# Scores of the first 22 chunks as spread tiles with a second mix, loads of the first batch in halves, and a shorter first AV and F1 part

## The chip, the cores and the metric

The kernel runs on one core of a Trainium2 chip. The metric is the device time of one execution, in microseconds (us). The core's engines run their own instruction lists side by side and wait for each other by semaphores: TensorE (PE, with its weight loads PEld), VectorE (DVE), ScalarE (ACT), GpSimd (POOL) and SyncE (SP). Most loads are issued by POOL, the moves between on-chip tiles by SP.

## The reference

Talking-heads attention over 8 batches of 12 heads, 448 positions and 64 dimensions, and then a feed-forward network with a squared ReLU (d_model 768, d_ff 2048). The two small 12x12 matrices mix the heads before and after the softmax.

```python
scores = scale * np.matmul(q, k.transpose(0, 1, 3, 2))
scores = np.einsum('bhij,hg->bgij', scores, w_pre)
scores = scores - np.max(scores, axis=-1, keepdims=True)
attn = np.exp(scores)
attn = attn / (np.sum(attn, axis=-1, keepdims=True) + 1e-09)
attn = np.einsum('bhij,hg->bgij', attn, w_post)
out = np.matmul(attn, v)
x = out.transpose(0, 2, 1, 3).reshape(B * S, H * D)
h = np.maximum(x @ w_in, 0.0)
return h * h @ w_out
```

## The kernel before

Each batch's 448 query positions are cut into 45 chunks of 10 (CH; ND = 22 and NCH = 45 count chunks). A chunk's 10 positions times 12 heads make 120 rows of a tile, so one matmul with a block matrix of w_pre mixes the heads of a chunk.

The work of PE is made of units, and the units form ten streams, by the digits of the string ORDER: 0 transposes of q and k (T), 1 scores q k^T (QK), 2 the mix with w_pre (pre), 3 the mix with w_post together with a transposition (post), 4 attention times v (AV), 5 direct scores of the first chunks (dir), 6 and 7 the first feed-forward product (F1), 8 and 9 the second (F2). ORDER gives the order of PE's units by hand; within a stream they run in the order in which the program makes them. A planner in the program (`_Plan`, costs written beside each task) takes PE's order as given, places the work of the other engines around it, gives evictions marked FLEX to DVE or ACT, whichever is done first, and puts warm-up matmuls (L649) into early gaps of PE. PE's order is fixed in the program that results: a unit that waits holds back those behind it.

The usual way of a chunk is long: QK (L974, or L986 in 64x64 tiles) writes scores into PSUM, DVE or ACT copies them to `stage` (L526, L527), SP moves each chunk's rows by DMA into `dring` (L1029), pre (L1052) mixes them, ACT takes exp with its row sums (L1070) into `pring`, DVE inverts the sums (L1094), POOL (DVE for the first chunks) folds them into the w_post block (L1101), post (L1133) writes the mixed attention, and DVE or ACT copies it to `a2t`. Then AV (L1211), F1 (L1257, later L1278 and L1292), relu and square, and F2 (L1413, L1427).

The first batch does its first 22 chunks on another way, without `stage` and `dring`: `emit_scale` (L900, on DVE) multiplies q by w_pre for every output head and writes the scaled q into the still unused `w_out_sb` (16 chunks) and `h2t` (6 chunks); `emit_direct` (L922) then needs six full 128x128 matmuls of 448 columns per chunk, one for each pair of heads, and exp reads their sum from PSUM. `wq` (L613), made from `wall`, holds the scaled w_pre, and `init9` (L882, ACT) clears the rows of padding. The w_out loads (`emit_load_w(1, ...)`) wait until the 16 chunks have left `w_out_sb`.

The loads of the first batch: the first q comes by SP as float32 into `xt` and is cast (`first_q`), the other q and the three k by POOL with a cast on the way; then w_in's first quarter, v, q and k of batch 1, and the rest of w_in. `emit_T` transposes q or k of four heads by 28 small transposes (L821) and evicts them by two copies of 128x448 into `qkt`.

AV of the first batch has two parts, chunks 0 to 21 and 22 to 44 (PARTS0), and F1 one group for each.

Of the kernel before, what the change touches and what calls it, by code (L numbers as in the profile page):

```python
# [8 lines left out]
DT = mybir.dt  # L9
# [16 lines left out]
EVENTS = {"tr": 0.12, "qk": 0.72, "di": 0.2, "po": 0.61, "pr": 1.1, "av": 0.43, "o0": 0.43}  # L26
# [5 lines left out]
    "0001501510105151555555555555555551335510015555555553335510021551355553255310055511255321"  # L32
    "5551233232444133433367232276761132761316772121776333626422444333277721166331766111672227"
    "6633672033720921193932194002442002831831181218214338313812182128216661333662227776332276"
    "7633377412144331411762216776200227677333772338311821802083320026662422441761181118333831"
    "3831921292193342219321922393292194114442336316316136202072372273763336217227163360071002"
    "7183138112823811933292292191183328212833181424433434224441326213636131637112727200726162"
    "1727317200736336302091911291129128238331833182911292219233914244332422831831833284241244"
    "1236331617333701206362172373272373263001620062161271171291329223933913813382128121842144"
    "4338332842244421861162383163361173372721772007272172623636330064144422820081118139138139"  # L40
    "3319329229219223933811938318132842444132621621721726236316316337337272272761762821383388"
    "33832184244439382829229639363637672722767673386376474448767667677676767968989989889899"
# [329 lines left out]
def bass_talking_heads_attention__then__ffn_squared_relu_kernel(  # L372
# [19 lines left out]
    NDW = 16  # L392
    DH = 4
    NE = 6
    NQ0 = 2
    QT0 = tuple((CH * (ND + x * (NCH - ND) // NQ0),
# [13 lines left out]
    PARTS0 = ((0, HC[0]), (HC[0], NCH))  # L410
# [6 lines left out]
    with ExitStack() as es:  # L417
# [43 lines left out]
        wq = early_bf[:, 512:512 + NP * NR // 2].rearrange("p (n h a) -> p n h a", n=NP, h=H)  # L461
        wall = early[:, 512:512 + NP * 2 * H].rearrange("p (n x h) -> p n x h", n=NP, x=2)
# [21 lines left out]
        sem_hq = Sm("dhq")  # L484
# [3 lines left out]
        sem_wq = Sm("dwq")  # L488
# [34 lines left out]

        def copy(eng, en, o, i_):
            if en == ACT:
                return eng.activation(o, i_, AF.Copy)  # L526
            return eng.tensor_copy(o, i_)  # L527

        streams = [[] for _ in range(10)]
        plan.streams = streams  # L530
        s_T, s_QK, s_pre, s_post, s_AV, s_dir = streams[:6]
        s_F1, s_F2 = streams[6:8], streams[8:]
# [3 lines left out]
        def fn_init(eng, en):  # L536
            eng.memset(mask[:, :, :], 1.0)
            eng.memset(wk1[:, :], 0.0)
            eng.memset(wrep[:, :], 0.0)
            eng.memset(wk2b[:, :, :], 0.0)  # L540
            return eng.memset(ident[:, :], 0.0)
# [43 lines left out]
        t_zrow = add("zrow", DVE, lambda eng, en: eng.memset(zrow[0:R0, :], 0.0), [],  # L585
# [14 lines left out]
        def fn_wall(eng, en):  # L600
            src = bass.AP(w_pre.tensor, 0, [[0, 128], [1, H * H]])
            eng.dma_start(wall[:, :, :, :].rearrange("p a b c -> p (a b c)"), src).then_inc(
                sem_wq.handle, 16)
            return None

        t_wall = plan.add("wall", SP, fn_wall, [], {SP: (400.0, 5300.0)}, -1e6 - 1, sem_wq, 16)
        wq_of = []
        for kk in range(2):
            def fn_wq(eng, en, r0=kk * 64, kk=kk):
                r_ = None  # L610
                for u in range(2):
                    i_ = wall[r0:r0 + 64, kk:NP:2, u, :].unsqueeze(3).to_broadcast([64, 3, H, H5])
                    r_ = eng.tensor_scalar(wq[r0:r0 + 64, 3 * u:3 * u + 3, :, :], i_,  # L613
                                           scale, None, op0=ALU.mult)
                return r_

            wq_of.append(add("wq%d" % kk, DVE, fn_wq, [t_wall], {DVE: (560.0, 640.0)}, -2e6))
# [57 lines left out]
        def load_qk(b, a, x, u, deps, after, prio):  # L675
            raw, src = ((qraw, q), (kraw, k))[x]

            def fn(eng, en):
                h = b * H + 4 * a
                if b == 0:  # L680
                    i_ = bass.AP(src.tensor, h * S * D, [[2 * NT * D, 128], [1, 2 * NT * D]])
                    o = raw[:, 2 * a:2 * a + 2, :, :].rearrange("p c t d -> p (c t d)")
                else:
# [3 lines left out]
                eng.dma_start(o, i_).then_inc(sem_qk[a][x].handle, 16)  # L687

            return plan.add("ldqk%d_%d_%d_%d" % (b, a, x, u), POOL, fn, deps,
                            {POOL: (600.0, 0.0)}, prio, sem_qk[a][x], 16, after=after,  # L690
                            dma=("load", 700.0, 88.0) if b else ("load", 1100.0 if a else 2590.0, 165.0))

        def first_q():
            part = xt.bitcast(DT.float32)[:, 0:4, :].rearrange("p a s -> p (a s)")

            def fn(eng, en):
                i_ = bass.AP(q.tensor, 0, [[2 * NT * D, 128], [1, 2 * NT * D]])
                eng.dma_start(part, i_).then_inc(sem_hq.handle, 16)
                return None

            t = plan.add("hq", SP, fn, [], {SP: (400.0, 3400.0)}, -1e6 - 2, sem_hq, 16)
# [99 lines left out]
        def emit_T(b):  # L801
            pb = b % 2
            for a in range(3):
                g = _Group(2)
                trs = []
                for i, src in enumerate((qraw, kraw)):
# [30 lines left out]
                    if b:  # L837
                        continue
# [852 lines left out]
```

## Time and profile before

| | |
|---|---|
| median of 3 runs | 519.81 us (518.43 to 520.98) |
| span of the profiled execution | 520.6 us |
| granted TensorE clock, mean | 0.999 |
| PE busy | 505.5 us, 97% |
| ACT busy | 425.6 us, 82% |
| DVE busy | 398.7 us, 77% |
| HBM read, written | 45.70 MB, 11.01 MB |

The span runs from the first to the last instruction of the profiled execution. Matmuls are pipelined, so the duration of one (a mean of 354 ns for L922) is longer than its pitch from start to start; costs on PE have to be taken from start times. Busy time of an engine in a stretch counts overlapping instructions once. The chain of waits follows the work that ended last back to the start, and says for each piece what released it.

### The profile page before, as it was taken

The page shows a single profiled execution, that of the slowest core. Times are in us where ns is not written, and L with a number is a line of the kernel's source. Part 1 is how long each engine was busy: PE and PEld are TensorE (multiplying, and loading weights), DVE is VectorE, ACT ScalarE, POOL GpSimd, SP SyncE. Part 2 cuts the span into 40 slices and gives each one's busy share as a digit, 9 for nine tenths or more (in the row PEclk, how much of TensorE's full clock was granted, in tenths as well). Part 3 has the DMA queues.
Part 4 walks back from the last instruction along what each step waited for, and adds up shares of the span by engine and source line. Part 5 has one row for each costly group of instructions (what it writes and reads, how often), then busy time and mean ns, then how long its engine had stood idle before and what let it go on. Part 6 is the DMA issues. An engine that isn't in the chain of part 4 may idle for free.

```text
span 520.6 us, 25670 instructions
## 1 busy us (share of the span) xinstructions
PE 505.5 (97%) x10859; PEld 340.1 (65%) x10859; DVE 398.7 (77%) x1004; ACT 425.6 (82%) x1206; POOL 203.4 (39%) x404
## 2 busy tenths in 40 slices
PE   8999999899999999999999999999999999999996
PEld 4555777668766665667657665667666666678963
DVE  6967988789987869967997779976887669757430
ACT  4799999879998898989887999988788879878311
POOL 9914364325632384134622464225440333123010
PEclk9999999999999999999999999999999999999999
DMA  8999999646893699347974689457972568432013
GB/s 160 208 218 184 197 194 184 156 107 144 167 180 86 136 177 197 92 112 166 178 156 90 153 175 179 98 111 170 167 151 59 125 140 148 91 81 69 4 39 90
DMA packets 82724, 72.12 MB, mean 139 GB/s; under 512 B 13578, under 2 KB 80090, under 8 KB 82602
## 3 DMA queue, kind: packets, MB, share of 16 engines
q0 software_dynamic: 36944, 32.81, 38.5%
q1 hardware_dynamic: 45370, 37.38, 29.7%
q8 instruction: 89, 1.46, 1.1%
q14 instruction: 33, 0.27, 0.1%
q10 hardware_dynamic: 288, 0.20, 0.1%
HBM read 45.70 MB, written 11.01 MB: 109 GB/s over the span
## 4 chain that ended last, share of the span: by engine, by line
PE 92%; DMA 3%; DVE 2%; issue 2%; ACT 1%; POOL 0%; DVEq 0%
PE ps L1413 17%; PE ps L1278 12%; PE ps L1427 9%; PE ps L1292 9%; PE ps L1133 8%; PE ps L1052 8%; PE ps L1257 6%; PE ps L1211 6%; PE ps L922 5%; PE ps L974 4%; DMA dring<-stage 3%; PE ps L825 2%; PE ps L1362 2%; PE ps L986 2%; PE ps L649 1%
## 5 line engine op out<-in xcount | busy, mean ns | idle before, releaser
L1070 ACT ACTIVATE pring<-ps 128x448 bf16<-128x448 f32 x360 | 192.0, 550 | 12.6 <-PE ps L1052 7.3
L1101 POOL TENSOR_TENSOR wk2s<-wk2b,rinv 128x120 bf16<-128x120 bf16 (+1 forms) x179 | 69.0, 389 | 223.5 <-DVE rinv L1094 222.8
L527 DVE CAST a2t<-ps 128x480 bf16<-128x480 f32 (+1 forms) x201 | 122.1, 640 | 18.4 <-PE ps L1133 16.9
L527 DVE CAST stage<-ps 128x448 bf16<-128x448 f32 (+1 forms) x189 | 112.8, 618 | 19.0 <-PE ps L986 8.7
L526 ACT ACTIVATE stage<-ps 128x448 bf16<-128x448 f32 (+1 forms) x171 | 87.9, 549 | 18.2 <-PE ps L986 10.6
L526 ACT ACTIVATE a2t<-ps 128x480 bf16<-128x480 f32 x167 | 88.2, 570 | 15.5 <-PE ps L1133 15.0
L1413 PE MATMUL ps<-w_out_sb,h2t 64*128 64x384 bf16 x1056 | 95.9, 322 | 0.0
L1070 ACT ACTIVATION_READ_ACCUMULATOR pring<-ps 128x1 f32 x360 | 76.9, 214 | 0.0
L1133 PEld LDWEIGHTS ps<-wk2s,pring 60*128 60x128 bf16 x2880 | 54.9, 93 | 24.7 <-issue 5.8
L1278 PE MATMUL ps<-xt,w_in_sb 64*128 64x448 bf16 (+2 forms) x840 | 70.6, 309 | 0.0
L1413 PEld LDWEIGHTS ps<-w_out_sb,h2t 64*128 64x128 bf16 x1056 | 48.4, 94 | 31.1 <-PE ps L1052 0.7
L1459 POOL DMA_DIRECT2D out_dram<-osb x59 | 36.9, 632 | 75.9 <-DVE osb L527 25.8
L1133 PE MATMUL ps<-wk2s,pring 60*128 60x60 bf16 x2880 | 62.3, 187 | 1.9 <-issue 1.4
L1052 PE MATMUL ps<-dring,wk 64*64 64x448 bf16 (+1 forms) x676 | 61.5, 359 | 2.4 <-issue 1.2
L1427 PE MATMUL ps<-w_out_sb,h2t 64*64 64x384 bf16 x1216 | 57.4, 323 | 0.9 <-issue 0.8
L1323 DVE TENSOR_SCALAR h1t<-ps 128x448 bf16<-128x448 f32 (+2 forms) x96 | 46.2, 488 | 12.6 <-PE ps L1278 9.1
L1292 PE MATMUL ps<-xt,w_in_sb 64*64 64x448 bf16 (+1 forms) x1008 | 54.5, 345 | 0.8 <-issue 0.6
L1332 DVE TENSOR_TENSOR h2t<-h1t 128x448 bf16<-128x448 bf16 (+2 forms) x176 | 52.0, 331 | 1.4 <-ACT h1t L1322 0.9
L1322 ACT ACTIVATE h1t<-ps 128x448 bf16<-128x448 f32 (+2 forms) x80 | 35.4, 448 | 19.7 <-PE ps L1278 13.9
L1094 DVE RECIPROCAL rinv<-rowsum 128x2 f32<-128x2 f32 (+1 forms) x184 | 29.3, 160 | 28.2 <-ACT pring L1070 27.1
L1278 PEld LDWEIGHTS ps<-xt,w_in_sb 64*128 64x128 bf16 x840 | 38.3, 94 | 18.1 <-DVE rinv L1094 0.5
L1427 PEld LDWEIGHTS ps<-w_out_sb,h2t 64*64 64x64 bf16 x1216 | 38.2, 107 | 13.8 <-issue 2.0
(70 smaller groups left out, 595.0 us busy)
## 6 DMA issues: line engine op xcount, KB each, us to landing
dring<-stage SPq DMA_DIRECT2D x309, 105.0 KB
out_dram<-osb POOLq DMA_DIRECT2D x45, 192.0 KB, 3.7
qraw<-in_q_dram POOLq DMA_DIRECT2D x42, 112.0 KB, 5.3
kraw<-in_k_dram POOLq DMA_DIRECT2D x42, 112.0 KB, 6.2
w_in_sb<-in_moe_w_in_dram POOLq DMA_DIRECT2D x8, 384.0 KB, 16.3
w_out_sb<-in_moe_w_out_dram POOLq DMA_DIRECT2D x8, 384.0 KB, 11.9
vraw<-in_v_dram POOLq DMA_DIRECT2D x21, 128.0 KB, 4.8
vraw<-in_v_dram POOLq DMA_DIRECT2D x21, 96.0 KB, 5.0
```

The costliest lines, as they stand in the source:

```text
L526: return eng.activation(o, i_, AF.Copy)
L527: return eng.tensor_copy(o, i_)
L1052: r_ = eng.matmul(ps[64 * y:64 * y + 64, gr.banks[x], 0:S], wk1[64 * x:64 * x + 64 - R0 * x, :], dring[64 * x:64 * x + 64 - R0 * x, (g0 + ...
L1070: return eng.activation(pring[:, pr, 0:S], ps[:, gr.banks[x], 0:S], AF.Exp, accum_out=rowsum[:, rs, :])
L1101: return eng.tensor_tensor(wk2s[:, p0:p0 + n, :], i0.to_broadcast([128, n, PR]), rinv[:, p0:p0 + n, :].to_broadcast([128, n, PR]), ALU.mult)
L1133: r_ = eng.matmul(ps[:, gr.banks[x], o0:o0 + PR], pring[64 * x:64 * x + PR, pr + y, j0:j0 + 2 * PJ], wk2s[64 * x:64 * x + PR, pr + y, :], ...
L1278: r_ = eng.matmul(ps[:, g.banks[x], 0:n], w_in_sb[64 * y:64 * y + 64, ft, t * 128:(t + 1) * 128], xt[64 * y:64 * y + 64, ft, c0:c1], start ...
L1292: r_ = eng.matmul(ps[64 * z:64 * z + 64, g.banks[x], 0:n], w_in_sb[64 * y:64 * y + 64, ft, t:t + 64], xt[64 * y:64 * y + 64, ft, c0:c1], s ...
L1323: return eng.tensor_scalar(h1t[:, box[0], 0:n], ps[:, g.banks[x], 0:n], 0.0, None, op0=ALU.max)
L1332: return eng.tensor_tensor(h2t[:, t16, o0:o0 + n], h1t[:, box[0], 0:n], h1t[:, box[0], 0:n], ALU.mult)
L1413: r_ = eng.matmul(ps[:, g.banks[hh], 0:FH], h2t[64 * y:64 * y + 64, t16, col:col + 128], w_out_sb[64 * y:64 * y + 64, t16, hh * FH:(hh + 1 ...
L1427: r_ = eng.matmul(ps[64 * z:64 * z + 64, g.banks[hh], 0:FH], h2t[64 * y:64 * y + 64, t16, col + 64 * z:col + 64 * z + 64], w_out_sb[64 * y ...
```

## The change

Spread scores. `emit_scale`, `emit_direct`, `wq` and `wall` go. The transposed q of the first 22 chunks is evicted straight into `qs`, in `w_out_sb`, where each chunk has four column strips of 32: ten columns for each of three heads, with zeros at the places that don't belong to a strip's head. `emit_spread` makes per chunk eight matmuls of 128 rows and 32 columns (sx, stream 5), which leave the scores of the twelve heads in four strips of one PSUM bank, one eviction `sv` of 128x448 on DVE or ACT into `sring` (8 slots), and one full matmul with `wks`, a block matrix of w_pre (mx, a new stream a). exp reads mx's result.

Loads. q of the first batch comes in halves, the first ones (the first seven of the fourteen positions that a partition holds, which become the first 224 columns) among the k, the second ones after all k; the first half q and the first k come by SP as float32 and are cast; eight small DMAs (`wreps`) replace `wall`. Then `EARLY`: w_in's first quarter, v, q and k of batch 1, the rest of w_in. w_out's loads wait for the mx of all 22 chunks. The output rows of the first batch are permuted to suit.

Parts. AV of the first batch has three parts, chunks 0 to 13, 14 to 21 and 22 to 44, and F1 two groups, the first of 14 chunks (140 columns), the second of the rest (308 columns).

ORDER is another one, of 967 units for 966; some costs of the planner are changed.

```diff
+TL = 4
+EARLY = ("w0", "v", "qk0", "qk1", "qk2", "w1", "w2", "w3")
-PARTS0 = ((0, HC[0]), (HC[0], NCH))
+PARTS0 = ((0, 14), (14, HC[0]), (HC[0], NCH))
+GROUPS0 = (PARTS0[:1], PARTS0[1:])
...
 ORDER = (
-    "0001501510105151555555555555555551335510015555555553335510021551355553255310055511255321"
-    "5551233232444133433367232276761132761316772121776333626422444333277721166331766111672227"
...
+    "00000000115015111155555aaa15aaa555a15533aa5a55353aaa30aaa5533553444111aaa50240aaa7630713"
+    "2336661202047241134162217632427332337263327331637241144411162276773337226671316226613173"
...
+        def fn_wreps(eng, en):
+            for j in range(TL):
+                for c, n, h in ((0, 2, head(j, 0)), (2, 1, head(TL + j // 2, j % 2))):
+                    src = bass.AP(w_pre.tensor, h * H, [[2 * H, n], [0, CH], [1, H]])
+                    r0 = 32 * j + c * CH
+                    eng.dma_start(wreps[r0:r0 + n * CH, :], src).then_inc(sem_ws.handle, 16)
...
+        def fn_wks(eng, en):
+            r_ = None
+            for x in range(2):
+                o = wks[:, 64 * x:64 * x + PR].rearrange("p (b a) -> p b a", a=H5)
+                i0 = wreps[:, :].unsqueeze(2).to_broadcast([128, H, H5])
+                i1 = masks[:, x * H5:(x + 1) * H5].unsqueeze(1).to_broadcast([128, H, H5])
+                r_ = eng.scalar_tensor_tensor(o, i0, scale, i1, op0=ALU.mult, op1=ALU.mult)
+            return r_
...
+        def emit_load_qk(b, heads=range(3)):
+            n = 0
+            if b == 0:
+                for a, x, u in ((0, 0, 0), (0, 1, 0), (1, 0, 0), (1, 1, 0), (2, 0, 0), (2, 1, 0),
+                                (0, 0, 1), (1, 0, 1), (2, 0, 1)):
+                    if a == 0 and u == 0:
+                        t = first(x)
+                    else:
+                        t = load_qk(b, a, x, u, [], [chain["t"]], -1e7 + 2 * a + u)
+                        chain["t"] = t
+                    qk_tasks[(a, x, u)] = t
+                return
...
+        flat = w_out_sb[:, :, :].rearrange("p a b -> p (a b)")
+        nqs = ND * TL * 2 * 32
+        qs = flat[:, 0:nqs].rearrange("p (c j x k) -> p c j x k", j=TL, x=2, k=32)
+        sring = flat[:, nqs:nqs + NSR * S].rearrange("p (n s) -> p n s", n=NSR)
+        def fn_init9(eng, en):
+            z = zrow[:, 0:2].bitcast(DT.float32)
+            return eng.activation(flat[:, 0:nqs].bitcast(DT.float32),
+                                  z.to_broadcast([128, nqs // 2]), AF.Copy)
...
+                    def fn_ev(eng, en, u=u, p=p):
+                        r_ = None
+                        if ND * CH < w:
+                            r_ = copy(eng, en, qkt[:, 0, p, 0, ND * CH:w],
+                                      ps_bf[:, g.banks[0], u * w + ND * CH:(u + 1) * w])
+                        for x in range(2):
+                            rows = slice(64 * x, 64 * x + 64)
+                            j, part, o0 = (p, 0, x * CH) if p < TL else (
+                                2 * (p - TL) + x, 1, 2 * CH)
+                            r_ = copy(eng, en, qs[rows, :, j, part, o0:o0 + CH],
+                                      ps_bf[rows, g.banks[0], u * w:u * w + ND * CH].rearrange(
+                                          "p (c a) -> p c a", a=CH))
+                        return r_
...
+        def emit_spread(c):
+            g = _Group(1)
+            slot = c % NSR
+            def fn_sx(eng, en):
+                r_ = None
+                for part in range(2):
+                    for j in range(TL):
+                        p = TL + j // 2 if part else j
+                        r_ = eng.matmul(ps[32 * j:32 * j + 32, g.banks[0], 0:S],
+                                        qs[:, c, j, part, :], qkt[:, 0, p, 1, :],
+                                        start=(part == 0), stop=(part == 1))
+                return r_
+            t = unit(s_spr, "sx%d" % c, fn_sx,
+                     [trev[(0, p, 0)] for p in range(NP)] + [trev[(0, p)] for p in range(NP)],
+                     395.0, "c32", g, 2 * TL)
+            def fn_sv(eng, en):
+                return copy(eng, en, sring[:, slot, :], ps[:, g.banks[0], 0:S])
+            t_sv = add("sv%d" % c, FLEX, fn_sv, [t, dir_done.get(c - NSR)], c_ev(S), -500.0 + c)
+            g.readers[0].append(t_sv)
+            g2 = _Group(1)
+            def fn_mx(eng, en):
+                return eng.matmul(ps[:, g2.banks[0], 0:S], wks[:, :], sring[:, slot, :],
+                                  start=True, stop=True)
+            t_mx = unit(s_mix, "mx%d" % c, fn_mx, [t_sv, t_wks], 190.0, "full", g2, 1)
...
-                emit_load_w(1, [dir_done[c] for c in range(NDW)])
-                emit_load_v(b)
+                emit_load_w(1, [dir_done[c] for c in range(ND)])
...
-            groups = [(p,) for p in parts_of(b)] if b in split else [parts_of(b)]
+            groups = GROUPS0 if b == 0 else [(p,) for p in parts_of(b)] if b in split else [parts_of(b)]
```

More of the change, by code (lines that the diff above doesn't have):

```diff
@@ L539, in fn_init @@
             eng.memset(wrep[:, :], 0.0)
+            eng.memset(wreps[:, :], 0.0)
+            eng.memset(wks[:, :], 0.0)
             eng.memset(wk2b[:, :, :], 0.0)
@@ L676, in load_qk @@
             raw, src = ((qraw, q), (kraw, k))[x]
+            sem = sem_qr[a] if u and not b else sem_qk[a][x]
             def fn(eng, en):
@@ L686, in fn, with first @@
                     o = raw[64 * u:64 * u + 64, 2 * a:2 * a + 2, :, :]
[L687 removed]
+                eng.dma_start(o, i_).then_inc(sem.handle, 16)
             return plan.add("ldqk%d_%d_%d_%d" % (b, a, x, u), POOL, fn, deps,
[L690 to L694, printed above, removed]
+                            {POOL: (600.0, 0.0)}, prio, sem, 16, after=after,
+                            dma=("load", 1100.0, 165.0) if x and not b else ("load", 700.0, 88.0))
+        def first(x):
+            raw, src = ((qraw, q), (kraw, k))[x]
+            n = (2 - (x == 0)) * NT * D
+            c0 = x * NT * D
+            part = xt.bitcast(DT.float32)[:, :, :].rearrange("p a s -> p (a s)")[:, c0:c0 + n]
             def fn(eng, en):
[L697 to L701 removed]
+                i_ = bass.AP(src.tensor, 0, [[2 * NT * D, 128], [1, n]])
+                eng.dma_start(part, i_).then_inc(sem_hq[x].handle, 16)
+                return None
+            t = plan.add(("hq", "hk")[x], SP, fn, [], {SP: (400.0, 3000.0 + 1000.0 * x)}, -1e6 - 3 + x,
+                         sem_hq[x], 16)
             def fn_cast(eng, en):
[L704 to L707 removed]
+                return copy(eng, en, raw[:, 0:2 - (x == 0), :, :].rearrange("p c t d -> p (c t d)"),
+                            part)
+            return add("ldqkc_%d_0" % x, FLEX, fn_cast, [t],
+                       {ACT: (n / 1.0 + 50.0, n / 1.0 + 150.0), DVE: (n / 1.92 + 70.0, n / 1.92 + 190.0)}, -4e6)
         def rows_of(b):
@@ L801, in emit_T @@
         def emit_T(b):
             pb = b % 2
+            if b == 0:
+                for a in range(3):
+                    for i in range(2):
+                        emit_T0(a, i, 0)
+                    if a == 0:
+                        T_of["first"] = T_of[(0, 0, 0)]
+                for a in range(3):
+                    emit_T0(a, 0, 1)
+                return
             for a in range(3):
```

265 lines of the change are left out of this document (108 added, 157 removed).

## The prediction

> **What bounds the kernel now.** I read the busy times and the granted clock first, then the busy time in four stretches, cut where the first F1 unit (54.6 us) and the first F2 unit (90.3 us) start.
>
> ```profile
> span 520.6 us, 25670 instructions
> PE 505.5 (97%) x10859; PEld 340.1 (65%) x10859; DVE 398.7 (77%) x1004; ACT 425.6 (82%) x1206; POOL 203.4 (39%) x404
> PE 92%; DMA 3%; DVE 2%; issue 2%; ACT 1%; POOL 0%; DVEq 0%
> 0.00:10.00 10.00, 8.03 (x103) 3.84 (x103) 5.76 (x24) 2.60 (x4) 8.78 (x21) 1.00 0.79 145
> 10.00:90.30 80.30, 77.87 (x1412) 50.29 (x1413) 67.33 (x198) 73.30 (x214) 40.59 (x75) 1.00 1.12 198
> 90.30:500.00 409.70, 404.00 (x9241) 276.99 (x9230) 324.52 (x784) 346.74 (x984) 151.46 (x305) 1.00 0.63 130
> 35.00:75.00 40.00, 38.95 (x734) 26.58 (x731) 33.02 (x90) 38.90 (x121) 17.00 (x34) 1.00 1.06 189
> ```
>
> The columns of a stretch are its length, then PE, PEld, DVE, ACT and POOL busy, the clock, the DMA share and GB/s. The reader is to see two things. PE is busy 97% and makes 92% of the chain of waits, so the kernel is bound by TensorE. But between 10.0 and 90.3 us DVE and ACT together are busy 67.33 + 73.30 = 140.6 of 2 x 80.3 us, 88%, and between 35 and 75 us (33.02 + 38.90) / 80 = 90%. After 90.3 us they are at 82%. So in the stage that the change rewrites a second bound lies close behind the first. Up to the first F2 unit both orders contain nearly the same other work (counted from the two ORDER strings: 30 QK units each, 23 pre units against 22, 32 post against 31), and afterwards they run alike. I therefore ask one question: when does the first F2 unit start, at 90.3 us now?
>
> **What the change takes from PE.** Start times in the timeline of PE give the pitch of a matmul and the price of a change of tile shape:
>
> ```profile
> 22.82 1.31 PE L922 MATMUL ps<-qkt,w_out_sb 128*128 128x448 bf16 x6
> 24.06 0.38 PE L986 MATMUL ps<-qkt 64*64 64x448 bf16 x4
> 24.28 0.39 PE L825 MATMUL ps<-ident,qraw 64*64 64x64 bf16 x28
> 25.12 5.28 PE L922 MATMUL ps<-qkt,w_out_sb 128*128 128x448 bf16 x27
> 30.33 0.84 PE L1133 MATMUL ps<-wk2s,pring 60*128 60x60 bf16 x48
> 70.44 2.15 PE L1211 MATMUL ps<-a2t,vraw 128*64 128x228 bf16 x40
> 72.53 0.65 PE L1133 MATMUL ps<-wk2s,pring 60*128 60x60 bf16 x34
> L922 PE MATMUL ps<-qkt,w_out_sb 128*128 128x448 bf16 x96 | 19.9, 354 | 0.3 <-DVE qkt L527 0.3
> L922 PE MATMUL ps<-qkt,h2t 128*128 128x448 bf16 x36 | 7.7, 354 | 0.0
> ```
>
> Six matmuls and a switch take 24.06 - 22.82 = 1.24 us, 27 and a switch 30.33 - 25.12 = 5.21 us. So one matmul takes 3.97 / 21 = 0.189 us and a switch 0.106 us. The direct scores (L922) are 96 + 36 = 132 matmuls: 132 x 0.189 = 24.9 us.
>
> A chunk now takes eight matmuls on 32 columns of the array (sx) and one full matmul (mx). No row shows 32-column tiles. The nearest are two: four 64x64 tiles with 448 columns take 24.28 - 24.06 = 0.22 us together, so four tiles do run at once, and forty 128x64 matmuls of 228 columns take 2.09 - 0.106 = 1.98 us, 0.050 each, half of what 0.189 x 228 / 448 = 0.096 would be alone, so column tiles halve the time. Bounds for the eight sx: four at a time 2 x 0.189 = 0.38 us, two at a time 0.76, one at a time 1.51. I take 0.40, near the four-tile row. Then 22 x (0.40 + 0.189) = 13.0 us replace 24.9: -11.9.
>
> It adds switches. Going through the two strings and counting changes of tile shape up to the first F2 unit gives 75 before and 96 after, since sx, mx and post follow each other in short blocks: 21 x 0.106 = +2.2 us. Splitting the first AV part in two adds four units at little more than the same columns; with its extra start terms and pieces I put +0.3. PE's own sum is -11.9 + 2.2 + 0.3 = -9.4: without any new wait the first F2 unit would start at 80.9 us.
>
> **What it does to DVE and ACT.**
>
> ```profile
> L900 DVE TENSOR_TENSOR w_out_sb<-qkt,osb 128x480 bf16<-128x480 bf16 x24 | 9.4, 448 | 0.1
> L900 DVE TENSOR_TENSOR h2t<-qkt,osb 128x480 bf16<-128x480 bf16 x6 | 2.6, 450 | 0.0
> L900 DVE TENSOR_TENSOR h2t<-qkt,osb 128x240 bf16<-128x240 bf16 x6 | 1.4, 304 | 0.0
> 17.11 2.98 DVE L900 TENSOR_TENSOR w_out_sb<-qkt,osb 128x480 bf16<-128x480 bf16 x8
> L613 DVE TENSOR_SCALAR osb<-osb 64x180 bf16<-64x180 f32 x4 | 1.2, 328 | 0.0
> 11.68 2.29 ACT L526 ACTIVATE stage<-ps 128x448 bf16<-128x448 f32 x5
> L527 DVE CAST stage<-ps 128x448 bf16<-128x448 f32 x20 | 12.0, 616 | 3.4 <-PE ps L986 1.8 <-DMA dring<-stage 0.9 <-PE ps L974 0.7
> L527 DVE COPY qkt<-ps 128x448 bf16<-128x448 bf16 x11 | 3.9, 383 | 1.2 <-PE ps L821 1.2
> L527 DVE COPY qkt<-ps 128x896 bf16<-128x896 bf16 x3 | 1.9, 617 | 0.0
> L527 DVE CAST qraw<-xt 128x896 bf16<-128x896 f32 x1 | 0.6, 628 | 1.5 <-DMA xt<-in_q_dram 1.5
> ```
>
> Out: eight scalings in 2.98 us are 0.372 each, the six half ones in proportion 0.25: 30 x 0.372 + 6 x 0.25 = 12.7 us, and 1.2 us of wq (L613). In: 22 evictions sv of 128x448; the same copy takes 2.29 / 5 = 0.46 us on ACT and at most 0.616 on DVE, I take 0.52: +11.4. The evictions of the transposes: k as before, q's first half in three pieces and three rests instead of six copies of 0.383. From 0.383 at 448 and 0.617 at 896 columns a piece of 220 takes 0.26, one of 4 about 0.15: 6 x (0.26 + 0.26 + 0.15) + 3 x 0.38 - 6 x 0.38 = +2.9. k's cast is +0.63, q's half cast saves 0.2, three more xt evictions about +0.4. Sum: -13.9 + 11.4 + 2.9 + 0.8 = **+1.2 us**. The one pre and one post unit fewer ahead of F2 take 2.2 us away (two exps, two evictions), which are paid later, where DVE and ACT have 18% free. init9 clears 2,816 float32 columns on ACT instead of 1,056 bfloat16 ones, before ACT has other work; bounds 0 and its full 2 us.
>
> So DVE and ACT have about 140 us to do from 10 us to the first F2. At full use that ends at 80.0, at 95% at 83.7, at 92.5% at 85.7, at 90% at 87.8 and at today's 88% at 89.5. PE's floor (80.9) lies below all but the first. I take 92.5%, a little over the 90% that these engines reached between 35 and 75 us while PE was what everybody waited for:
>
> ```profile
> 18.59 0.55 ACT L1070 ACTIVATE pring<-ps 128x448 bf16<-128x448 f32 x1 [2.44 <-PE ps L922]
> 10.00:20.00 10.00, 9.83 (x135) 4.96 (x136) 9.96 (x31) 6.82 (x17) 10.00 (x18) 1.00 1.35 200
> ```
>
> The first exp waits 2.44 us for L922 and ACT is busy 6.82 of 10 us there. sx needs every q half and every k, but no scaling, and less data lies ahead of the third k (three q halves are put behind it), so I expect the first exp some 4 us earlier. First F2 then at 85.7, -4.6, with 0.4 paid back for the deferred units: **-4.2 us**. Against the profiled span: 520.6 - 4.2 = 516.4. The span lies 0.8 above the median of the runs, 519.81, so the forecast is **515.6**.
>
> **Edits that I cost at nothing.** EARLY only reorders loads, and F1 waits for none of them today; w_out's loads now wait for all 22 chunks, not 16.
>
> ```profile
> L753 POOL DMA_DIRECT2D w_out_sb<-in_moe_w_out_dram x8: 752/794/801, 38.2 to 62.8; - x8
> DMA to landing us min/median/max: 9.7/11.9/14.8
> 54.65 1.30 PE L1257 MATMUL ps<-xt,w_in_sb 128*128 128x220 bf16 x12
> 90.31 1.50 PE L1427 MATMUL ps<-w_out_sb,h2t 64*64 64x384 bf16 x32
> ```
>
> The last w_out load is issued at 62.8 and lands by 62.8 + 14.8 = 77.6 at the latest, 12.7 us ahead of F2. F2 comes 4.6 us earlier and the first load some 5 us later (the 22nd mx stands just ahead of the first F1 unit), which leaves a few us; gone, that cover would cost what is missing of it. The small SP loads wreps stand ahead of zdma and wsmall, first needed by pre, after 30 us.
>
> [...] A 128x64 tile's weight loads stand beside a full tile's:
>
> ```profile
> L1211 PEld LDWEIGHTS ps<-a2t,vraw 128*64 128x64 bf16 x80 | 3.7, 109 | 0.6 <-issue 0.5
> L922 PEld LDWEIGHTS ps<-qkt,w_out_sb 128*128 128x128 bf16 x96 | 8.5, 98 | 8.7 <-ACT stage L526 0.6 <-DVE qkt L527 0.5 <-issue 0.4
> ```
>
> They take 0.109 against 0.098 us, and at 0.050 us per matmul they overlap each other. [...]
>
> **The rivals.**
> A, forecast: DVE and ACT packed to between 90.6 and 95%: 517.2 down to 513.6. Chance 0.43.
> B: they pack nearly fully (or I counted too much) and PE's floor decides: -6 to -9: 510.5 to 513.5. For it: in 35 to 75 us ACT alone is at 97%. 0.14.
> C: evacuation stays near today's 88% (519.4 by the same sum), the extra copies eat what PE gives up: 517.2 to 520.5. 0.22.
> D: sx runs two at a time, by streams or by weight loads: 22 x 0.36 = 7.9 of the 9.4 us are gone, PE's floor is 88.8: about 518.7. 0.08; one at a time: 22 x 1.11 = 24.4, less 9.4: 535. 0.02.
> E, slower: a new wait. PE runs in a fixed order, and each mx waits for its sv, which queues on DVE or ACT behind exps and copies; whatever follows on PE waits too. The 22 mx stand in 11 blocks. An sv takes 0.46 to 0.62 us plus its queue. If each block stalls PE by 0.85 us, the 9.4 us are gone: that is the point from which it decides. At 1.4 us it is 11 x 1.4 - 9.4 = +6 us: 526. For it: only one to five sx stand between an sx and its mx. Against: 0.4 us each of cover, and other units between. 0.11.
>
> **How the numbers follow.** A measurement tells 0.5%, 2.6 us, from no change: 517.2 to 522.4. Faster: A and B, 0.57. Same: C and most of D, 0.30. Slower: E and the rest of D, 0.13. The range leaves out E, the serial case and the lowest edge: 510.5 to 521.
>
> **What will show it.** First F2 at 85 to 87 us; sx units 0.38 to 0.44 us from start to start; DVE and ACT together over 90% between 10 us and the first F2, and PE now idle there by some 5 us more; first exp near 14 us. PEld or PE waiting for DVE or ACT at mx for over 8 us in all speaks for E; sx at 0.76 for D. I am wrong at the root if the first F2 starts earlier and the end does not follow.

## The result, and the profile after

| | before | after |
|---|---|---|
| median of 6 runs each, on one chip | 519.62 us (518.15 to 520.98) | 527.42 us (523.17 to 531.97) |
| span of the profiled execution | 520.6 us | 530.2 us |
| first F2 unit starts | 90.31 us | 95.34 us |
| from there to the end | 430.3 us | 434.9 us |

The ratio after to before is 1.0112, 95% interval 1.0068 to 1.0157: the change makes the kernel 1.1% slower. Here and below a median takes all runs and a ratio only those within 1.5% of the fastest of their kernel, so the ratio can lie below (or above) the quotient of the medians. The forecast was 515.6 us. The profiled execution is the longest of the six, so its ledger (+9.6 us) is larger than that of the medians (+7.8 us).

The head of the page of the kernel after, and its share of the chain of waits by engine:

```profile
span 530.2 us, 25701 instructions
PE 501.8 (95%) x10873; PEld 328.9 (62%) x10873; DVE 404.8 (76%) x1013; ACT 420.4 (79%) x1202; POOL 204.9 (39%) x406
...
PE 79%; ACT 6%; DMA 5%; DVE 4%; issue 3%; SPq 1%; POOL 0%; DVEq 0%; ACTq 0%
```

PE is busy 3.7 us less than before, in a span that is 9.6 us longer. So PE did get less work, and lost the gain and more in gaps. The stretches of the kernel after say where (length, then PE, PEld, DVE, ACT and POOL busy, the clock, the DMA share and GB/s):

```profile
10.00:20.00 10.00, 5.68 (x79) 2.09 (x79) 5.24 (x15) 3.07 (x7) 10.00 (x19) 0.73 1.37 198
24.00:43.20 19.20, 18.49 (x412) 8.93 (x413) 17.25 (x42) 19.12 (x61) 3.33 (x7) 1.00 1.05 198
50.00:75.00 25.00, 19.58 (x436) 12.89 (x434) 18.90 (x62) 20.07 (x63) 9.45 (x19) 0.93 0.98 164
10.00:95.30 85.30, 73.49 (x1391) 41.73 (x1393) 67.01 (x189) 70.22 (x208) 40.49 (x75) 0.94 1.03 182
```

The same stretches before:

```profile
24.00:43.20 19.20, 19.20 (x372) 10.30 (x371) 12.60 (x35) 17.86 (x50) 4.60 (x10) 1.00 1.17 211
50.00:75.00 25.00, 24.22 (x482) 19.27 (x479) 22.09 (x64) 24.24 (x76) 10.98 (x22) 1.00 1.06 194
```

Between 24 and 43 us the new order does what it was forecast to do: PE gets through 412 matmuls for 372, and DVE and ACT together are busy 36.4 of 38.4 us, 95%, against 79% before. On either side lies a hole. From 10 to 20 us PE is busy 5.68 us, for 9.83 before, and at a clock of 0.73; from 50 to 75 us it is busy 19.6 for 24.2.

**The first hole** stands in the timeline (start, length, engine, line, operation and tile; in brackets the idle time before, and its releaser), here rows of SP, DVE, PE and ACT in the kernel after:

```profile
1.75 6.10 SPq L614 DMA_DIRECT2D osb<-in_w_pre_dram  x8
...
13.29 0.35 DVE L633 SCALAR_TENSOR_TENSOR osb<-osb 128x60 bf16<-128x60 f32 x2 [3.99 <-DMA osb<-in_w_pre_dram]
...
15.36 0.96 PE L1038 MATMUL ps<-qkt 64*64 64x448 bf16 x8 [3.94 <-DVE qkt L534]
...
16.00 0.98 ACT L533 ACTIVATE stage<-ps 128x448 bf16<-128x448 f32 x2 [6.92 <-PE ps L1038]
```

Read it from the top. SP takes 6.10 us to issue the eight small loads of `wreps`, 0.76 us each. DVE reaches wks (L633) at 9.30 and stands there for 3.99 us until they land. The evictions of transposed q and k are queued behind wks on DVE; QK on PE waits 3.94 us for one of them, and ACT 6.92 us for QK. The clock falls to 0.5 at 14.6 us and stays there for 6.8 us. The first mx, the first user of wks, starts only at 22.96 us.

**The second hole** has no engine as its releaser. PE in the kernel after:

```profile
46.04 0.25 PE L934 MATMUL ps<-ident,kraw 64*64 64x64 bf16 x7 [1.33 <-issue]
...
55.24 0.38 PE L1105 MATMUL ps<-dring,wk 64*64 64x448 bf16 x2 [3.95 <-issue]
...
109.61 0.19 PE L934 MATMUL ps<-ident,kraw 64*64 64x64 bf16 x1 [2.60 <-issue]
```

These units waited for nothing that the profile shows. I numbered PE's records (matmuls and weight loads) by start time, from 0: all three units begin, with the matmul or its weight load, at number 193 of a block of 256. On queue q8, which the page calls "instruction" (89 packets, 1.46 MB: 16,384 bytes each), the trace has a packet shortly ahead of each such end. My own count from the trace, us (idle time at a block end is taken from the start of the record before, so it is 0.2 to 0.4 us more than in the rows above):

```
block reached   idle ahead of it   next packet on q8   from block to packet
before  40.24        0.00             44.06-44.94            3.82
before  47.92        0.01             51.57-52.50            3.65
before  53.90        0.72             58.07-59.02            4.17
after   34.14        0.00             38.57-39.46            4.44
after   41.02        0.32             43.62-44.50            2.60
after   46.04        1.52             52.87-53.81            6.83
after   55.24        4.33             57.34-58.28            2.10
```

I read it so, though the trace records no request: on entering a block PE asks for a later one, and cannot enter the next before that packet has landed and 1.4 us more have gone by (53.81 to 55.24). Below, a packet is "asked for" when PE reaches the block. Before, a block lasts 7.4 to 8.1 us at 24 to 48 us, and a packet comes 3.5 to 4.1 us after it was asked for: enough. The new order gets through 256 records in 5 to 7 us, and a packet took up to 6.8. Idle times over 0.3 us at such block ends add up to 16.5 us in the kernel after, 6.9 of them ahead of the first F2, and to 8.4 and 1.2 us before.

So two theories stand for the experiments: **W**, the wait of wks on DVE, and **F**, late instruction fetches in a denser PE order. The rival of both is that the order itself is no denser, or that mx, sx or the evictions set the pace.

### The profile page after: what moved, and what is told of

Same layout as the page of the kernel before. It is cut to its first block, busy times and chain, and to the rows that moved or that the text cites. A ratio compares the mean times of both kernels' runs of the same rounds, so it can differ in the third digit from the quotient of the medians.

```text
span 530.2 us, 25701 instructions
## 1 busy us (share of the span) xinstructions
PE 501.8 (95%) x10873; PEld 328.9 (62%) x10873; DVE 404.8 (76%) x1013; ACT 420.4 (79%) x1202; POOL 204.9 (39%) x406
## 3 DMA queue, kind: packets, MB, share of 16 engines
q8 instruction: 89, 1.46, 1.1%
## 4 chain that ended last, share of the span: by engine, by line
PE 79%; ACT 6%; DMA 5%; DVE 4%; issue 3%; SPq 1%; POOL 0%; DVEq 0%; ACTq 0%
PE ps L1466 16%; PE ps L1331 12%; PE ps L1480 8%; PE ps L1186 7%; PE ps L1105 7%; PE ps L1264 6%; PE ps L1310 6%; PE ps L1345 5%; PE ps L1026 4%; DMA dring<-stage 4%; ACT pring L1123 3%; PE ps L1415 2%; PE ps L1038 2%; PE ps L934 2%; DVE a2t L534 1%
## 5 line engine op out<-in xcount | busy, mean ns | idle before, releaser
L534 DVE CAST stage<-ps 128x448 bf16<-128x448 f32 (+1 forms) x215 | 127.9, 617 | 19.1 <-PE ps L1026 8.3
L534 DVE CAST a2t<-ps 128x480 bf16<-128x480 f32 x196 | 119.0, 640 | 13.5 <-PE ps L1186 12.8
L533 ACT ACTIVATE a2t<-ps 128x480 bf16<-128x480 f32 (+1 forms) x172 | 91.7, 583 | 16.8 <-PE ps L1186 16.5
L533 ACT ACTIVATE stage<-ps 128x448 bf16<-128x448 f32 (+1 forms) x145 | 75.5, 547 | 21.3 <-PE ps L1038 10.7
L1123 ACT ACTIVATION_READ_ACCUMULATOR pring<-ps 128x1 f32 x360 | 79.9, 222 | 0.0
L1331 PE MATMUL ps<-xt,w_in_sb 64*128 64x448 bf16 (+2 forms) x912 | 77.0, 311 | 0.0
L1105 PE MATMUL ps<-dring,wk 64*64 64x448 bf16 (+1 forms) x676 | 60.7, 362 | 6.5 <-issue 4.4
L1375 ACT ACTIVATE h1t<-ps 128x448 bf16<-128x448 f32 (+4 forms) x87 | 38.8, 454 | 21.9 <-PE ps L1331 14.3
L1385 DVE TENSOR_TENSOR h2t<-h1t 128x448 bf16<-128x448 bf16 (+4 forms) x176 | 53.2, 332 | 1.8 <-ACT h1t L1375 1.2
L1376 DVE TENSOR_SCALAR h1t<-ps 128x448 bf16<-128x448 f32 (+4 forms) x89 | 42.9, 486 | 13.5 <-PE ps L1331 8.0
L1345 PE MATMUL ps<-xt,w_in_sb 64*64 64x448 bf16 (+1 forms) x864 | 46.3, 347 | 0.0
## 6 DMA issues: line engine op xcount, KB each, us to landing
w_in_sb<-in_moe_w_in_dram POOLq DMA_DIRECT2D x8, 384.0 KB, 11.9
```

The source lines that it names most:

```text
L1105: r_ = eng.matmul(ps[64 * y:64 * y + 64, gr.banks[x], 0:S], wk1[64 * x:64 * x + 64 - R0 * x, :], dring[64 * x:64 * x + 64 - R0 * x, (g0 + ...
L1123: return eng.activation(pring[:, pr, 0:S], ps[:, gr.banks[x], 0:S], AF.Exp, accum_out=rowsum[:, rs, :])
L1331: r_ = eng.matmul(ps[:, g.banks[x], 0:n], w_in_sb[64 * y:64 * y + 64, ft, t * 128:(t + 1) * 128], xt[64 * y:64 * y + 64, ft, c0:c1], start ...
L1345: r_ = eng.matmul(ps[64 * z:64 * z + 64, g.banks[x], 0:n], w_in_sb[64 * y:64 * y + 64, ft, t:t + 64], xt[64 * y:64 * y + 64, ft, c0:c1], s ...
L1376: return eng.tensor_scalar(h1t[:, box[0], 0:n], ps[:, g.banks[x], 0:n], 0.0, None, op0=ALU.max)
L1385: return eng.tensor_tensor(h2t[:, t16, o0:o0 + n], h1t[:, box[0], 0:n], h1t[:, box[0], 0:n], ALU.mult)
```

## The experiments

Each was timed beside the kernel before on the same chip. "Block ends" are PE's idle times over 0.3 us at block ends ahead of the first F2, in the profiled execution.

| kernel | median, us | ratio to before (95%) | first F2 | block ends |
|---|---|---|---|---|
| after | 527.42 | 1.0112 (1.0068 to 1.0157) | 95.34 | 6.9 |
| wks late | 524.79 | 1.0062 (1.0022 to 1.0102) | 89.00 | 6.3 |
| wks late, PE order shifted by 64 instructions | 523.32 | 1.0028 (0.9982 to 1.0074) | 89.06 | 7.1 |
| before, with an unused wks | 526.02 | 1.0093 (1.0050 to 1.0136) | 93.42 | 0 |
| before, direct scores in strips | 526.96 | 1.0141 (1.0090 to 1.0192) | 98.26 | 11.6 |
| wks late, w_out late | 535.25 | 1.0289 (1.0247 to 1.0332) | 91.82 | 4.3 |
| wks late, fewer transposes | 524.13 | 1.0022 (0.9978 to 1.0065) | 90.78 | 3.9 |
| wks mid | 523.78 | 1.0022 (0.9980 to 1.0064) | 89.55 | 7.2 |
| wks mid, fewer transposes | 524.29 | 1.0037 (0.9999 to 1.0074) | 87.08 | 3.3 |
| wks mid, w_out cut | 518.51 | 0.9936 (0.9901 to 0.9971) | 86.28 | 4.0 |
| before, w_out cut | 518.69 | 0.9962 (0.9933 to 0.9990) | 87.67 | 0 |
| wks mid, w_out and w_in cut | 520.13 | 0.9936 (0.9885 to 0.9986) | 84.57 | 2.9 |
| before, w_out and w_in cut | 517.78 | 0.9961 (0.9936 to 0.9985) | 87.40 | 0 |

The runs of a changed kernel lie further apart than those of before (wks mid with both cuts: 511.87 to 526.78 us, the kernel before beside it 516.62 to 524.18). The first F2 and the block ends are of one execution each.

### The kernel after once more

> The changed kernel itself, unaltered, for a second profile. Theory W (the wait of wks on DVE for the small loads, with PE idle 3.94 us behind it, is built into the program): the same wait stands at the same place, 3 to 5 us on DVE, and PE idles 3 to 5 us from about 11 us. Theory F (instruction fetch of PE, 16 KB at a time, comes late in the denser order): the stalls marked issue lie again at the same PE instructions (every 256th), but their lengths vary; in the first profile those over 0.3 us came to 16.6 us against 8.4 us in the kernel before. Rival N (the first profile was an unlucky run): both are gone and the span is near 518 us.

It took 981.67 us: in this one execution PE took about twice as long for its matmuls (24 of sx and a switch in 2.51 us, 1.25 in the profile of the result), so its time says nothing of the change. Two things in it still bear on the theories. wks waited for its loads again:

```profile
12.93 0.35 DVE L633 SCALAR_TENSOR_TENSOR osb<-osb 128x60 bf16<-128x60 f32 x2 [2.65 <-DMA osb<-in_w_pre_dram]
...
15.01 0.87 PE L1038 MATMUL ps<-qkt 64*64 64x448 bf16 x8 [2.35 <-DVE qkt L534]
```

And with PE half as fast through its blocks, the block ends add up to 0.77 us in the whole execution, against 16.5.

### W: wks moved to just ahead of the first mx

```diff
+        committed.remove(t_wks)
+        committed.insert(next(i for i, t in enumerate(committed) if t.name == "mx0"), t_wks)
```

> The changed kernel with one DVE operation, wks, moved behind the early evictions and copies, directly ahead of the first mx in the order of the program; nothing else is altered. Theory W: DVE no longer stands still at about 9.3 us, PE's idle time of 3.94 us before the first QK falls below 1 us, the granted clock does not halve for the 6.8 us behind it, first F2 about 6 us earlier than 95.3 us, and the time falls by 5 to 8 us, to some 520 us. Rival F (fetch stalls are the larger part): under 3 us gained. Rival of the PE floor (sx and mx do not pay): first F2 stays after 90.3 us even without stalls.

PE in this kernel:

```profile
11.49 0.57 PE L1038 MATMUL ps<-qkt 64*64 64x448 bf16 x8 [0.67 <-DVE qkt L534]
...
17.60 0.73 PE L985 MATMUL ps<-w_out_sb,osb 128*128 128x448 bf16 x3 [0.93 <-DVE wk L642]
...
42.94 0.25 PE L934 MATMUL ps<-ident,kraw 64*64 64x64 bf16 x7 [3.25 <-issue]
...
50.36 0.38 PE L1105 MATMUL ps<-dring,wk 64*64 64x448 bf16 x2 [1.65 <-issue]
```

The wait of 3.94 us is down to 0.67, the clock stays at 1 until 43 us, and the first F2 starts at 89.00, 6.3 us earlier. The first mx still waits 0.93 us (its row names L642, the operation right behind wks on DVE). The block ends stay: 0.8, 3.4 and 2.0 us, the last two at the same units as before the edit (L934 with seven transposes, L1105 with two pre). So W is real, and it is not all: the kernel is still 0.6% above before. The time fell by 2.6 us (527.42 to 524.79) and not by the 5 to 8 expected; under 3 us was the sign set for F.

### W in the kernel before

The kernel before gets the eight loads on SP and a wks on DVE ahead of its third scaling; nothing uses the result.

```diff
...
+        t_wreps = plan.add("wreps", SP, fn_wreps, [t_init], {}, 0.0, sem_ws, 128)
+        t_wks = add("wks", DVE, fn_wks, [t_wreps, t_init], {}, 0.0)
+        put(t_wreps, [t for t in committed if t.engine == SP][2])
+        put(t_wks, [t for t in committed if t.name.startswith("sc")][2])
```

> The kernel before with the eight small loads put into SP's queue behind its first two loads and a wks of the same form (its result is used by nothing) put on DVE behind the third scaling. Theory W: DVE waits there for the small loads, 3 to 5 us, the scalings and evictions of the transposes behind it are late, and the kernel gets slower by 2 to 6 us (PE has fewer warm-ups to bridge it, so the clock may halve too). Rival: the wait is covered by other work and the time stays within 0.5%.

DVE and PE in this kernel:

```profile
12.92 0.35 DVE L1569 SCALAR_TENSOR_TENSOR osb<-osb 128x60 bf16<-128x60 f32 x2 [3.96 <-DMA osb<-in_w_pre_dram]
...
13.99 0.93 PE L926 MATMUL ps<-qkt,w_out_sb 128*128 128x448 bf16 x2 [4.38 <-DVE qkt L530]
```

The same wait (3.96 us), the same gap on PE (4.38), the same 6.8 us at half clock, and 526.02 us for 521.10: **+4.9 us** from these instructions alone, without a spread score in the program.

### F: does the stall go with the unit or with the count?

To the kernel with wks late, the first block of warm-up matmuls becomes four full ones and 37 of 16 columns: 64 PE instructions more, little time.

```diff
...
-                for _ in range(n):
+                big = 4 if first and n >= 9 else n
+                for i in range(n + 32 if big < n else n):
+                    w = S if i < big else 16
...
```

> As the kernel with wks late, and the first block of warm-up matmuls holds 4 of 448 columns and 37 of 16 instead of 9 of 448, so that PE has 64 more instructions ahead of all its work. Theory F: the stalls marked issue move to units 64 instructions earlier in the order and stay at multiples of 256 instructions of PE counted from the start; the time may go either way by 2 to 3 us as the stalls meet other units. Rival (a stall belongs to its unit, pre or T, by something that the profile does not show): the stalls stay at the same units as with wks late.

PE in this kernel:

```profile
33.62 0.56 PE L1270 MATMUL ps<-a2t,vraw 128*64 128x140 bf16 x12 [0.98 <-issue]
...
45.90 0.37 PE L1111 MATMUL ps<-dring,wk 60*64 60x448 bf16 x1 [1.44 <-issue]
```

Other units stall now, AV at 33.62 and another pre at 45.90, and each is again number 193 of its block. The stalls belong to the count of instructions and not to what the units wait for. Their sum is as large (7.1 for 6.3 us), so a luckier cut alone brings nothing.

### F in the kernel before

Each full matmul of the direct scores becomes four of 32 columns: 792 PE instructions more (matmuls and weight loads), while PE's busy time from 10 us to the first F2 only grows from 77.87 to 78.46 us, so four of them run in about the time of one.

```diff
+                    w4 = qs[:, p, y:y + 2, :].rearrange("p i g -> p (i g)")
+                    for z in range(0, 128, 32):
+                        r_ = eng.matmul(ps[z:z + 32, g.banks[0], 0:S], w4[:, z:z + 32],
+                                        qkt[:, 0, p, 1, :],
...
```

> The kernel before, each of the 132 direct matmuls cut into four matmuls on 32 columns of the array: the same sums, the same work on DVE, ACT and DMA, 792 more instructions on PE, no q scaling removed. Theory F (the fetch of PE's instructions, 256 at a time, takes 6 to 9 us while the queues are full of loads, so a stage with more instructions per us starves PE): 3.1 blocks more between 10 and 47 us, a block then lasts some 5 us on PE, stalls marked issue of 8 to 15 us appear there, and the time rises by 6 to 14 us. Rival (instruction count is harmless, the stalls of the changed kernel come from the units that follow): four strips take 0.19 us as one matmul did, and the time rises by under 2 us.

What PE waited for between 10 and 98 us (total us, times, longest):

```profile
PE ps L825 <- issue: 4.1, 2, 2.5
PE ps L924 <- issue: 2.4, 2, 1.8
PE ps L1212 <- issue: 1.7, 1, 1.7
PE ps L1134 <- issue: 0.8, 1, 0.8
PE ps L975 <- issue: 0.7, 1, 0.7
```

Seven block ends idle before the first F2, 11.6 us of them, and the first F2 is 8.0 us late; the time is 526.96 for 519.95. Loads, order and units are those of before. So F stands by itself as well: shorter PE instructions in the same stage cost 1.4%.

### What makes the fetch late: w_out's loads issued later

In the kernel with wks late the eight w_out loads move from 40.7 to 61.8 us to 58.0 to 63.7 us, behind folds of chunks 37 to 43.

```diff
+        late = [t for t in committed if t.name.startswith("ldw1_")]
...
+        for n, t in enumerate(late):
+            at = "fold0_%d" % (37 + n // 2 * 2)
+            committed.insert(next(i for i, u in enumerate(committed) if u.name == at) + 1, t)
```

> The kernel with wks late, and the eight loads of w_out issued behind the folds of chunks 37 to 43 instead of from 40.7 us on; every other order is the same. Theory F with loads as its cause: the fetches at 36 to 50 us, which waited 4.6 to 5.2 us for their packet, wait 1 to 3 us, the stalls there (0.8, 3.4 and 2.0 us) shrink to under 2 us together, the clock stays up, and the time falls by 3 to 6 us below wks late. Rival (the fetch is late whatever POOL has queued, the moves and the small packets are enough): the same stalls, time within 1.5 us. Rival D (w_out comes too late for F2): first F2 later than 89 us, slower.

A miss for the time, but not for the question. Packets asked for at 43, 48 and 55 us come after 2.8, 1.1 and 1.1 us (with wks late alone, those asked for at 43 and 50: 5.2 and 1.3), and the stall near 50 us is gone. Those at 36.0 and 43.0 stay (0.8 and 3.4 us): their packets were asked for at 28.7 and 36.0, behind w_in's loads (issued from 21.2 to 25.9 us). Where the moved loads now stand it is the other way round: the packet asked for at 59.7 took 5.8 us, and with wks late alone the one asked for at 61.1 took 2.7. The first F2 comes 2.8 us later than with wks late; ahead of it the clock is at half for 6.8 us from 64.4 on, behind a wait of 1.4 us on PE. And the q of batch 2, issued behind the loads put together at 58, lands 17.9 us after its issue in the median, for 7.0 with wks late:

```profile
PE ps L934 <- DMA qraw<-in_q_dram: 9.3, 1, 9.3
```

One wait of 9.3 us after the first F2 has begun, and 10.2 us at half clock from 98.5 on: more than the stall that went.

### Fewer instructions: transposes of 128 columns

Batches 1 and 2 transpose by 14 matmuls of 128 columns in place of 28 small ones per group, 168 PE instructions fewer for a batch.

```diff
...
-                        for t in range(NT):
+                        for t in range(NT if thin else 0):
+                            o = (POS[t] if i else t) * 128
+                            for c in range(2):
+                                r_ = eng.transpose(ps_bf[64 * c:64 * c + 64, g.banks[i], o:o + 128],
+                                                   src[:, 2 * a + c, t, :], ident[:, :])
...
```

> The kernel with wks late, with the transposes of batches 1 and 2 made by 14 matmuls of 128 columns a unit instead of 28 of 64 (two evictions in place of one, ordered one behind the other): 168 instructions fewer on PE in each of the two batches, just where its stalls lie, for about 1.1 us more of PE work a batch. Theory F: one block lasts longer than 56 of its instructions in 0.4 us, the stalls at 43, 50 and 103 us shrink by 3 to 6 us in all, net 1 to 4 us faster than wks late. Rival (stalls don't come from the number of instructions): 1 to 3 us slower by the added work.

The stalls are smaller (3.9 for 6.3 us), but the first F2 comes at 90.78 and not earlier than 89.00: PE is busy 75.20 us from 10 us to the first F2, for 70.49 with wks late. That holds the longer transposes and two stretches of 3.4 us at half clock for one; I did not separate them. With wks placed as in the next kernel:

> wks mid together with the thinner transposes of batches 1 and 2, the best combination so far of what the runs showed. Theory F: 0.5 to 1.5 us below the kernel with thin transposes and wks late (ratio 1.0022), so within 0.3% of the kernel before, perhaps a little faster; it does not reach the forecast of 0.8% faster, since the loads still delay the fetch.

The first F2 is at 87.08, 3.2 us ahead of before; the time is 0.4% above before, at the edge of what can be told from it, and not below the kernel with fewer transposes and wks late, as was expected.

### wks six copies earlier

```diff
+        committed.remove(t_wks)
+        at = next(i for i, t in enumerate(committed) if t.name == "mx0")
+        committed.insert([i for i, t in enumerate(committed[:at]) if t.engine == DVE][-6], t_wks)
```

> As wks late, with wks five copies earlier on DVE: behind the landing of its loads (13.3 us in the changed kernel's profile) and ahead of the first mx. Theory W: PE's remaining wait at the first mx (0.93 us with wks late) falls under 0.3 us, time 0.5 to 1.5 us below wks late. Theory F: the rest of the way to the forecast stays lost, the stalls marked issue between 30 and 60 us again sum to 4 to 7 us, so it ends within 1% of the kernel before.

In the trace wks stands six copies ahead of its place with wks late. The 0.93 us that mx waited are gone, and the first F2 is no earlier (89.55 for 89.00), behind 7.2 us of block ends (3.4 at 42.8). The time, 523.78, can't be told from before.

### The loads taken out

Of w_out's first three quarters three rows in four are not loaded, and F2 multiplies what lies there. The same in the kernel before is the control.

```diff
+                            n = nt if j == 3 else 1
...
+                                          [[F, 128], [128 * F, n], [1, wc]])
+                            dst = w_out_sb[:, j * nt:j * nt + n, x * wc:(x + 1) * wc]
```

> As wks mid, but of w_out's first three quarters only a fourth is loaded (the rest of that tile keeps what lies there; F2 multiplies it all the same), so 1.4 of 3.1 MB remain in the queues between 40 and 70 us. Theory F (the fetch is late because of the loads, and only that hides what PE gave up): fetches after 42 us wait 0.5 to 3 us, stalls there under 2 us, first F2 at 82 to 86 us, time 513 to 517 us, 4 to 8 us below its control with the same cut in the kernel before. Rival A2 (DVE and ACT are full, so PE could not have gained more): first F2 stays at 88 us or later with few stalls and DVE and ACT over 92% busy from 10 us on.

> The kernel before with the same cut of w_out's loads (three quarters of its first three quarters left out; F2 multiplies what lies there): the control. Its PE needs a block of 256 instructions only every 7.5 us up to 48 us, so both theories expect little: 0 to 2 us faster than the kernel before.

Two stalls of 2.0 us are left, at 40.0 and 47.6, and none from there to 149. The first F2 is 3.3 us earlier than with the loads, but the control gains 2.6 as well (90.31 to 87.67; 1.2 of them its own block ends). So the first F2 lies 1.4 us ahead of the control's, and the median only 0.2 us below its median, where 4 to 8 were expected; the two ratios can't be told apart. The packet behind the second stall was asked for at 40.0 and took 5.3 us. So two thirds of w_in's last three quarters are left out too, in both kernels; F1 multiplies the loaded rows again in their place.

> The kernel with wks placed mid-way and three of four rows of w_out's first three quarters not loaded (518.51 us, first F2 at 86.28, two stalls of 2.0 us at 40 and 47.6 and 3.4 us at half clock), and now also two thirds of w_in's last three quarters not loaded; F1 multiplies the loaded rows again in their place, so the products are others. Fetch theory: what is left of the delay at 36 to 48 us comes from fetches that queue behind w_in's loads; with these gone the packet asked for at 40 us comes within 3.5 us instead of 5.3, the two stalls fall below 0.5 us each, the clock stays at 1, and the first F2 starts at 81 to 84 us (2 to 5 us earlier). Rival, order theory: the stalls vanish and the first F2 stays at 85.5 to 86.5, since exps and evictions set the pace. Rival, queue theory wrong: the stalls at 40 and 47 stay near 2 us with fetches as late as before.

> Control: the kernel before with the same loads of w_out and w_in left out (without the cut of w_in 518.69 us and first F2 at 87.67). It had no stall over 0.3 us between 10 and 87 us, so all theories expect little: first F2 at 87 to 87.7 us, time within 0.3% of 518.7. Fetch theory: the kernel of the other run is then 3 to 6 us (0.6 to 1.1%) below this one; order theory: 1 to 2 us below; queue theory wrong: about 1 us below, as before.

Stretches of the changed kernel with both cuts, and of its control with the last row:

```profile
42.00:84.60 42.60, 41.30 (x796) 26.51 (x788) 38.26 (x115) 41.31 (x129) 20.27 (x41) 1.00 0.85 152
10.00:84.60 74.60, 69.87 (x1419) 40.82 (x1413) 66.06 (x189) 69.12 (x208) 38.05 (x75) 1.00 0.92 163
```

```profile
10.00:87.40 77.40, 76.97 (x1414) 49.89 (x1412) 67.10 (x197) 72.67 (x214) 38.07 (x75) 1.00 0.92 165
```

The packet asked for at 40.96 comes after 2.2 us for 5.3, the stall behind it is gone, and the clock stays at 1 up to the first F2. Two stalls are left, 1.1 and 1.8 us at 35.7 and 41.0, whose packets were asked for at 28.0 and 35.7 and took 5.2 and 2.8 us; so the theory of the fetches was right in direction and too hopeful in size (stalls under 0.5 us and a first F2 by 84 were expected). The first F2 starts at 84.57, 2.8 us ahead of the control, and after the stalls, from 42 us, DVE and ACT together are busy 93%. But the end doesn't follow: a stall of 2.8 us at 98.1 and 3.4 us at half clock come after the first F2, and the medians are 520.13 and 517.78, with ratios whose intervals overlap, where 3 to 6 us below the control were expected.

## Why the prediction was wrong

**The step that failed** is the price of nothing on the small loads: "The small SP loads wreps stand ahead of zdma and wsmall, first needed by pre, after 30 us". It prices what wreps holds up in SP's queue, and not the instruction that waits for wreps itself: wks. wks stands early on DVE, and every eviction behind it waits. The program gives it the planner priority of the first tasks (-2e6) and takes the loads to have landed 6.5 us after their start; they landed after 11.5 us (1.75 to 13.29). The prediction had to ask which instruction waits for each load, on which engine, and what is queued behind. Costed at nothing, it measured 4.9 us in the kernel before, and 6.3 us at the first F2 of the kernel after (95.34 to 89.00), of which 2.6 us came back in the time.

**What was left out** is the instruction fetch. The sum of PE went by time alone; that the same time holds more instructions had no price. The kernel itself has one: its planner, the same before and after, counts PE's instructions in blocks of 256 from an offset of 63 (`BLOCK`, `fetch`), so that a block ends at number 193, and allows at most 5.45 us from entering one block to the next; where a block end stalled, up to 9.2 us passed (46.04 to 55.24). In the kernel before, with its direct scores in strips, it cost 1.4% by itself. In the kernel with wks late, 6.3 us of stalls and 3.4 us at half clock lie ahead of a first F2 that is 3.3 us behind the forecast of 85.7.

Point by point:
- PE's sum, -9.4 us: near, but too large. PE is busy 69.87 us from 10 us to the first F2 with wks mid and both cuts, 8.0 us less than before (77.87) and 7.1 less than in its control (76.97). An sx was taken at 0.40 us. In the rows below 24 matmuls and a switch take 26.34 - 25.09 = 1.25 us, so eight take (1.25 - 0.106) / 3 = 0.38 us. Rival D, two at a time, is out.

```profile
25.09 1.32 PE L968 MATMUL ps<-qkt,w_out_sb 128*32 128x448 bf16 x24
26.34 0.36 PE L985 MATMUL ps<-w_out_sb,osb 128*128 128x448 bf16 x1
```

- The sum of DVE and ACT, about 140 us: too high by 3 to 5. It is 66.37 + 69.66 = 136.0 us with wks late, 135.2 with both cuts. Which of its terms was too large I did not settle; sv was not (22 evictions take 6.1 + 6.9 = 13.0 us, for 11.4).
- Both engines packed to 92.5%: right where neither W nor F acts (95% from 24 to 43 us, 93% from 42 us on with both cuts), wrong for the stage: (67.01 + 70.22) / 170.6 = 80% in the kernel after.
- First exp near 14 us: wrong. It starts at 23.52, and without W still at 17.99, 0.6 us earlier than before.
- w_out's loads later at no cost: right for F2, which waits for no load. But these loads, and w_in's, go along with late fetches: with both cuts the packets asked for from 41 us on came in 0.6 to 3.6 us, up to the first F2.
- "Afterwards they run alike": off by 4.6 us in the profiled executions, where block ends after the first F2 hold 9.7 us for 7.3, and 3.4 us from 110.2 run at half clock. But that execution is the longest of its kernel; from the first F2 on, wks late takes 432.1 and wks mid 430.6 us, for 430.3 before. The sign that the prediction named for being wrong at the root does show: wks late, wks mid, and wks mid with fewer transposes start F2 0.8 to 3.2 us earlier than before, and none ends earlier (ratios 1.0062, 1.0022 and 1.0037). So one question, when F2 starts, was not enough.
- Rival E gave 526, near the 527.42 measured, which is luck: its mechanism is a wait of mx for sv, and mx (L985) idles 0.1 us in all. A new wait did decide, in front of wks and not of mx.

What stays open: how far the order would get with no late fetch at all. With both cuts the first F2 is at 84.57 with 2.9 us of stalls ahead of it, so 82 us is argued and not shown. What exactly delays a packet is open too: taking loads away shortened most delays, yet 5.2 us were left at 28 us. And where gains ahead of the first F2 go afterwards is open: from there to the end the profiled executions take 430 to 435 us in the kernels of either order that are neither late in w_out nor thin in transposes. No version ran faster than before with all of its work.

## What to carry to other kernels

For each small load or constant that a change adds, follow it to the instruction that waits for it and price what is queued behind that instruction on its engine, not when the result is first used. When an edit replaces few long PE instructions by many short ones, count the instructions per microsecond beside the time: here PE had no stalls between 24 and 48 us at 256 records (matmuls and weight loads) in 7.4 us or more, and lost 6 us ahead of the first F2 at 5 to 7 us. Loads issued in bulk in such a stage belong into that sum: with both cuts the packet asked for at 40.96 us came after 2.2 us, and with all of w_in loaded the one asked for at 40.0 after 5.3.

## What the runs showed of the hardware

- PE's idle times of over 0.3 us put down to "issue" come at a fixed place in blocks of 256 records (within two of number 193; the one exception is 0.46 us with w_out late), and ahead of the first F2 they end 1.3 to 1.6 us after a packet of 16,384 bytes on the instruction queue; in the kernels before and after, those packets took from 1.1 to 6.8 us to come there.
- Half clock came in stretches of 3.4, 6.8 and 10.2 us around or after gaps on PE: 6.8 us with a gap of 3.9 (after, 14.6 us) and 4.4 (before with wks, 11.9 us), 3.4 after 4.3 at 55 us (after), 10.2 after 9.3 (w_out late, 98.5 us). Shorter gaps were followed by half clock in some cases (1.4 us at 63.8, w_out late: 6.8 us; 2.0 at 40.0, w_out cut: 3.4 us) and not in others (3.1 at 102.8, wks late), so the length of the gap alone does not tell.
- In the kernel after, eight DMAs of under 1 KB in a row took SP 6.1 us to issue, and the last landed 5.4 us after its issue ended, while the loads of q and k were on their way.
